# Idle products on TensorE, and a quarter of the last batch's spectral products on POOL

## The chip, the cores and the metric

The kernel runs on one core of a Trainium2 chip, in one launch. The metric is the device time of one execution in microseconds (us). Five engines work side by side, each through its own instructions in order: PE (TensorE, matrix products into PSUM), DVE (VectorE), ACT (ScalarE), POOL (GpSimd) and SP (SyncE, which here only issues DMAs).

## What is computed

For 8 batches of 3136 rows and 256 columns, an attention-like product without softmax feeds a gated long convolution:

```python
scores = matmul(z, z.T) / S                    # S = 3136, z has 64 columns
x      = u * matmul(maximum(scores, 0)**2, v)  # u, v: S x 256
x1, x2, x3 = split(x @ w_proj, 3)              # 256 columns each
conv = irfft(rfft(x2, axis=seq) * rfft(filter_fft, axis=seq))
out  = (x1 * conv * x3) @ w_out
```

Inputs and output are float32; the kernel works in bfloat16 with float32 accumulation.

## The kernel before

The sequence is cut into 7 chunks (`CHUNKS`). For each batch and chunk PE makes blocks of scores into PSUM (`ps_s`), ACT takes the positive part (`R_t`, L1767), DVE or ACT squares it (`A_t`, L1776 and L1774), and PE weighs `v` with it into `ps_o`. DVE multiplies the result by `u` (`xT_t`, L1818). With `wp` PE then makes two gate factors, which ACT copies (L554) and DVE multiplies (`gate_t`, L1160), and the input of the convolution.

The convolution is a transform of 3136 = 64 x 49 points, in two steps, with scratch in HBM (`spec`) between them for the reordering. `dft1` makes the first step. `add_spectrum` makes, for each of 8 groups of frequencies (`g`): the second step (`forward`, two PSUM banks), its eviction to a tile `xh` in SBUF (for the last batch `R_t` and `xh` by turns), the complex product with the filter's spectrum `H` on DVE (L1248), the first inverse step (`inverse`), its eviction, and a write to `spec`. `add_end` loads that back (`conv_in_t`; `A_t` for the last batch, L1006), makes the last inverse step (PE, `T`), multiplies it by the gate (`yT_t`, L1334), multiplies by `w_out` (`wo`), evicts and stores.

The complex product of a group is written as `mul(0)` and `mul(1)`: the spectrum tile (4 x 256 = 1024 elements in each of 128 partitions) times the real or the imaginary part of `H`. In batches 0 to 6 two additions (L1252, L1253) follow on DVE. In the last batch (`final`) they are left out and `inverse2` sums the parts in PSUM instead, with the negated matrices `minus`; there are 16 products of 1024 elements in that batch, all on DVE. The groups of the last batch run when no scores or weighing of another batch are left; in the batches before, they run between those of the following batch.

The order of instructions on every engine is not written by hand. A planner (`Plan`) holds queues of tasks with a cost, dependencies and buffers (`Slots`, `Pairs`, `Singles` for PSUM banks), steps through a time of its own, and at each step starts the task that can start first. PE's queues are S (scores), Q (second transform steps), W (weighing), FA, FB and FZ (projections and output). The times in the planner are guesses which only decide an order; on the chip, an instruction starts when its engine has come to it and its semaphores allow.

The lines that matter: `Plan.go` (L356) picks the next task; `mul` (L1245) with `w_` and `z_` (L1256 to L1258); `inv` (L1260), whose task waits for `z_`; `bank` (L532) gives the PSUM bank of a task; `matmul` (L520) records a product with its bank.

Of the kernel before, what the change touches and what calls it, by code (L numbers as in the profile page):

```python
# [12 lines left out]
P = 128  # L13
# [4 lines left out]
ALU = mybir.AluOpType  # L18
# [10 lines left out]
SPEC_LAG = 1  # L29
LATE_F = 6.0  # L30
LATE_OUT = 2.0
AFTER = (1, 3, 5, 6)
FINAL = (0, 2, 4, 6, 1, 3, 5)
ZP, ZL = 0, 0.0
# [10 lines left out]
def c_act(n):  # L45
    return 0.055 + n * 0.000833
# [6 lines left out]
def c_dve2(n):  # L53
    return 0.068 + n * 0.00052


def c_pe(*ns):
    return sum(n / 2400 + 0.003 for n in ns)
# [123 lines left out]
class Plan:  # L182
# [151 lines left out]
    def pick(self, e):  # L334
# [18 lines left out]
                best = (key, s, task)  # L353
        return best and (best[1], best[2], e)

    def go(self):  # L356
        while True:
            got = []
            x = self.pick_pe()
            if x:  # L360
                got.append((x[0], 0, x[1], "PE", x[2]))
            for i, e in enumerate(self.pend):
                x = self.pick(e)
                if x:
                    got.append((x[0], i + 1, x[1], e, None))
            if not got:
                break
            start, _, task, e, k = min(got, key=lambda g: g[:2])
            if k:
                self.queues[k].remove(task)  # L370
                half = k in ("S", "Q")
                if half != (self.mode == "S") and self.mode:
                    start += 0.096
                    self.quarters, self.quad_run, self.score_run = half and self.soon, 0, 0
                self.score_run += k == "S"
                if k == "Q":
                    self.quad_run += 1
                    if self.score_run and not self.quarters:
                        start += 0.092
                    self.quarters = True  # L380
                self.mode = "S" if half else k
                if k == "W":
                    self.credit = min(self.credit + self.rule(start).pace, 2.0)
                elif k != "S":
                    self.credit = max(self.credit - task.cost["PE"], -2.0)
            self.run(task, e, start)
        left = sum(len(q) for q in self.queues.values()) + sum(len(q) for q in self.pend.values())
        assert not left, f"{left} tasks left over"
# [3 lines left out]
def kernel(  # L392
# [10 lines left out]
    nc = tc.nc  # L403

    B, S, D = u.shape
# [23 lines left out]
    plan = Plan()  # L429
# [90 lines left out]
    def matmul(o, *args, **kw):  # L520
        wrote(nc.tensor.matmul(o, *args, **kw), o)  # L521
# [4 lines left out]
    pair_slots, one_slots, half_slots = Pairs(banks), Singles(banks), Halves(banks)  # L526
# [5 lines left out]
    def bank(dtype=F32):  # L532
        for p in ps_o:
            if plan.bank is p.slots:
                return p.tile()
        i, h = plan.got[0][1]
        x = ps_t[i][:, h, :]
        return x if dtype == F32 else x.bitcast(dtype)
# [9 lines left out]
    def on(engine, emit, cost, deps=(), takes=(), **kw):  # L548
        return job(None, lambda e: emit(), {engine: cost}, deps, takes, **kw)
# [75 lines left out]
    ident = const.tile([P, P], BF16, name="ident")  # L625
# [74 lines left out]
    plan.free["POOL"] = 12.0  # L700
    plan.free["SP"] = 3.0
    plan.free["DVE"] = 1.5


    def after(task, at):
# [12 lines left out]
    for i, (t0, t1) in enumerate(zip(z_cuts, z_cuts[1:])):  # L718
        step_ = -(-(t1 - t0) // -(-(t1 - t0) // 8))
        for g0 in range(t0, t1, step_):  # L720
# [15 lines left out]
            n = nt * dqk  # L736
            at = ZF_AT[i]
# [23 lines left out]
            ev = job(None, back, {"DVE": c_dve2(w), "ACT": c_act(w)}, [tt], prio=0)  # L761
# [17 lines left out]
    H = const.tile([P, NJ, 2, D], BF16, name="H")  # L779
# [163 lines left out]
    minus_task = []  # L943
# [129 lines left out]
    def c_quads(i, n=1):  # L1073
        return n * (1 if i else 2) * c_pe(2 * D) + 0.01
# [139 lines left out]
    def add_spectrum(b, puts):  # L1214
        deps0 = list(h_done) + list(tz_done) if b == 0 else []
        final = b == B - 1
        sets = [(0, 1), (2, 3), (4, 5), (6,), (7,)] if final else [(0, 1), (2, 3), (4, 5), (6, 7)]
        set_of = {g: x for x in sets for g in x}
        outs = [gs_p, gs_p, M_p[2], A_p, uT_p] if final else [gs_p] * 4
        homes = [l_p, l_p, *M_p[:2]]  # L1220
        lasts = []
        behind = []
        ldb, gb = [None], [None]
        for g in range(NJ // 2):
            own = not final or g % 2 == 0
            xh = xh_p if own else R_p
            mine = set_of[g]
            per, gh = 2 * len(mine), outs[sets.index(mine)]
            if g % 2 == 0:
                ldb[0] = load_spec(D1[b % 2], 2 * g, 4, puts, LATE_LOAD * (not final), homes[g // 2] if final else l_p)  # L1230
            ld, ibox = ldb[0]
            xb = {}

            def mm(ps, g=g, xb=xb, ibox=ibox, xh=xh):
                xb["x"] = xh.tile([P, 2, 4, D], BF16)
                forward(ps, slot(ibox["t"], 2 * g % 4), g)

            def ev(e, h, p, xb=xb):
                copy(e, xb["x"][:, 0, ds(2 * h, 2), :].rearrange("p c d -> p (c d)"), p)

            a0, evs = add_quads(mm, ev, c_quads(g), [ld, *deps0], [xh.slots])
            if g % 2:
                a0.frees.append((ld, 0))

            def mul(i, g=g, xb=xb):  # L1245
                x = xb["x"][:].rearrange("p i (j c) d -> p i j c d", c=2)
                h = H[:, ds(2 * g, 2), i].unsqueeze(2).to_broadcast([P, 2, 2, D])
                nc.vector.tensor_tensor(x[:, 1 - i], x[:, 0], h, ALU.mult)  # L1248

            def add(xb=xb):  # L1250
                x = xb["x"][:].rearrange("p i (j c) d -> p i c j d", c=2)
                nc.vector.tensor_tensor(x[:, 1, 0], x[:, 1, 0], x[:, 0, 1], ALU.subtract)  # L1252
                nc.vector.tensor_tensor(x[:, 1, 1], x[:, 1, 1], x[:, 0, 0], ALU.add)  # L1253

            cost = c_dve2(4 * D)
            w_ = on("DVE", lambda mul=mul: mul(0), cost, evs, prio=ZP)  # L1256
            w_ = on("DVE", lambda mul=mul: mul(1), cost, [w_], prio=ZP, lat=ZL)
            z_ = w_ if final else on("DVE", add, 2 * c_dve2(2 * D), [w_], prio=ZP)  # L1258

            def inv(g=g, xb=xb, z_=z_, a0=a0, gh=gh, mine=mine, per=per):  # L1260
                new = g == mine[0]
                if new:
                    gb[0] = {"es": [], "firsts": []}
                gx = gb[0]

                def mm(ps, g=g, new=new):
                    if new:
                        gx["g"] = gh.tile([P, 2 * per, D], BF16)
                    z, y = (slot(xb["x"][:, i], 0) for i in range(2))
                    if final:  # L1270
                        inverse2(ps, y, z, g)
                    else:
                        inverse(ps, y, g)

                def ev(e, h, p, g=g):
                    copy(e, gx["g"][:, ds(2 * (2 * (g - mine[0]) + h), 2), :].rearrange("p c d -> p (c d)"), p)

                a, evs = add_quads(
                    mm, ev, c_quads(g, 1 + final), [z_, *gx["firsts"], *(minus_task if final else [])], [gh.slots] if new else []
                )  # L1280
                gx["firsts"] = [a]
                if new:
                    gx["g0"] = a
                a.frees.append((a0, 1))
                inverses.append(a)
                gx["es"] += evs
                if g != mine[-1]:
                    return
                j0 = 2 * mine[0]

                def put():
                    for rows, part in by_row(D2[b % 2], gx["g"], 2 * j0, 2 * per):
                        nc.sync.dma_start(out=rows, in_=part)

                p_ = on("SP", put, 1.2, gx["es"], moves=0.5 * per, late=LATE_D2 * (not final))
                p_.frees.append((gx["g0"], 1))
                lasts.append(p_)

            behind.append(inv)
            if g >= SPEC_LAG:  # L1300
                behind.pop(0)()
        for x in behind:
            x()
        return lasts

    def add_end(b, lasts, gtasks, cs, kind="FB", src=c_p, dsts=(o_p,), late=0, behind=(), then=(), split=False, mids=(y_p,)):
        for at, c in enumerate(cs):
# [94 lines left out]
            else:  # L1402
                s_ = on("SP", lambda nt=nt, store=store: store(0, nt), 1.3, [*oe, *behind], prio=1, moves=0.45 * nt, late=LATE_OUT * (dst is o_p))
            s_.frees.append((o0, 1))
# [326 lines left out]
    for gi, g in enumerate(groups):  # L1731
        deps = []
        for un in g:
            b, c, k = un
# [7 lines left out]
        more = ends_at.get(gi, [])  # L1742
# [12 lines left out]
        for i, un in enumerate(g):  # L1755
            b, c, k = un
            cw = CHUNKS[c]
            pair = plans[b, c][k][1]
            rows, n = P, len(parts(un))
# [38 lines left out]
            if pair != (NT - 1,):  # L1798
                w_ = add_weigh(un, [q_], lambda t, q_=q_: t.frees.append((q_, 0)))
# [112 lines left out]
```

## Time and profile before

| | |
|---|---|
| three timed runs | 991.3, 991.36, 992.84 us; median 991.36 |
| profiled execution | 993.72 us, of which the span from the first to the last instruction 991.5 |
| busy share of the span | PE 97%, ACT 88%, DVE 83%, POOL 19% |
| mean granted clock of TensorE | 0.990 |
| instructions | 19534 in all, 6831 matrix products, 409 on POOL |

The page's lists and the answers of the trace give, for each group or instruction: source line, engine, operation, tiles out<-in, shape, count; then the busy time and mean duration in ns, and the idle time of the engine before it with what ended it. In the rows in order of time the first number is the start in us from the span's start, the second the time that the row covers. Helpers hold many operations: L521 is every matrix product, L554 and L558 every copy by ACT or DVE, so the tiles' names tell them apart.

### The profile page before, as it was taken

To read this page: it belongs to the slowest core of one execution; us is meant where nothing else is said; L and a number is where in the kernel's file an instruction comes from. 1 tells how busy PE (TensorE), PEld (TensorE's weight loads), DVE (VectorE), ACT (ScalarE), POOL (GpSimd) and SP (SyncE) were. 2 spreads that over 40 slices of the span, in tenths; PEclk is the share of its full clock that TensorE was granted. 3 is DMA by queue.
4 is the path that set the end of the run, shared out by engine and by line. 5 is a ranking of instruction groups with operands and counts; after the bars stand their busy time and mean duration, and the time that the engine had idled before them with its cause. 6 is when DMAs were issued, how large, how long until landed. Compare 5 with 4: busy or idle time off the path is not lost.

```text
span 991.5 us, 19534 instructions
## 1 busy us (share of the span) xinstructions
PE 958.2 (97%) x6831; PEld 472.2 (48%) x6831; DVE 819.4 (83%) x1465; ACT 867.9 (88%) x1187; POOL 191.7 (19%) x409
## 2 busy tenths in 40 slices
PE   6999999999999999999999999999999999999985
PEld 2344544455444554446444454444544455544643
DVE  7876689987899878987789877898779988799774
ACT  6988898988998898899989999889989899999773
POOL 5132311132013210313111220121202231001001
PEclk9999999999999999999999999999999999999978
DMA  9889958979979799978998786998889978984576
GB/s 154 150 171 199 165 118 128 187 137 185 202 174 176 147 194 187 186 156 133 200 197 178 148 152 152 205 191 158 153 196 186 203 138 165 202 213 106 154 229 197
DMA packets 332343, 170.32 MB, mean 172 GB/s; under 512 B 242442, under 2 KB 307786, under 8 KB 332244
## 3 DMA queue, kind: packets, MB, share of 16 engines
q1 hardware_dynamic: 304068, 136.59, 63.4%
q0 software_dynamic: 28176, 32.48, 23.2%
q8 instruction: 54, 0.88, 0.4%
q14 instruction: 45, 0.37, 0.1%
HBM read 90.26 MB, written 53.35 MB: 145 GB/s over the span
## 4 chain that ended last, share of the span: by engine, by line
PE 82%; DVE 7%; ACT 4%; DMA 2%; issue 2%; SPq 1%; POOL 0%; POOLq 0%; DVEq 0%; ACTq 0%
PE ps_o_t L521 48%; PE ps_s L521 34%; DVE A_t L1776 2%; ACT R_t L1767 2%; DVE xT_t L1818 1%; DMA M2e_t<-A_t 1%; DVE xh L1248 1%; DMA ost_t<-in_z_dram 1%; DMA conv_in_t<-spec 1%; DVE gate_t L1160 1%; DVE yT_t L1334 1%; SPq L646 1%; ACT A_t L1774 0%; ACT x_t L554 0%; DMA M_t<-A_t 0%
## 5 line engine op out<-in xcount | busy, mean ns | idle before, releaser
L1767 ACT ACTIVATE R_t<-ps_s 128x1024 f32<-128x1024 f32 (+4 forms) x512 | 466.9, 963 | 57.1 <-PE ps_s L521 55.0
L521 PE MATMUL ps_o_t<-A_t,v_t 128*128 128x512 bf16 (+3 forms) x2084 | 459.5, 354 | 2.9 <-DVE A_t L1776 2.1
L521 PEld LDWEIGHTS <-v_t 128*128 128x128 bf16 (+2 forms) x2878 | 250.6, 98 | 257.8 <-issue 73.2
L1776 DVE TENSOR_TENSOR A_t<-R_t 128x1024 bf16<-128x1024 f32 (+3 forms) x283 | 313.9, 1123 | 64.2 <-ACT R_t L1767 61.1
L1774 ACT ACTIVATE A_t<-R_t 128x1024 bf16<-128x1024 f32 (+3 forms) x213 | 211.7, 1007 | 3.1 <-DMA M2e_t<-A_t 1.7
L521 PE MATMUL ps_s<-zT_t 64*64 64x512 bf16 (+5 forms) x1485 | 170.8, 361 | 2.0 <-ACT R_t L1767 1.0
L604 POOL COPY tick<-xT_t 1x1 bf16<-1x1 bf16 x54 | 13.8, 256 | 681.6 <-DVE xT_t L1818 681.6
L521 PEld LDWEIGHTS <-zT_t 64*64 64x64 bf16 (+1 forms) x1518 | 53.9, 101 | 109.7 <-issue 93.7
L521 PE MATMUL ps_s<-xT_t,wp 128*128 128x512 bf16 (+2 forms) x430 | 103.7, 353 | 2.4 <-DVE gate_t L1160 0.9
L554 ACT ACTIVATE x_t<-ps_s 128x512 bf16<-128x512 f32 (+2 forms) x148 | 81.7, 583 | 19.7 <-PE ps_s L521 12.5
L1818 DVE SCALAR_TENSOR_TENSOR xT_t<-ps_o_t,uT_t 128x256 bf16<-128x256 f32 (+2 forms) x224 | 76.1, 381 | 22.8 <-PE ps_o_t L521 14.4
L1248 DVE TENSOR_TENSOR xh<-xh,H 128x1024 bf16<-128x1024 bf16 x120 | 82.0, 683 | 2.1 <-ACT xh L554 0.9
L521 PE MATMUL ps_o_t<-M_t,v_t 128*128 128x512 bf16 (+2 forms) x352 | 81.8, 353 | 0.0
L1160 DVE TENSOR_TENSOR gate_t<-ps_s,x_t 128x256 bf16<-128x256 f32 (+2 forms) x216 | 71.2, 381 | 6.6 <-PE ps_s L521 4.6
L1334 DVE TENSOR_TENSOR yT_t<-ps_s,gate_t 128x512 bf16<-128x512 f32 (+2 forms) x99 | 57.9, 613 | 10.3 <-PE ps_s L521 10.0
L558 DVE CAST xh<-ps_s 128x512 bf16<-128x512 f32 x71 | 47.3, 685 | 22.8 <-PE ps_s L521 19.5
L521 PEld LDWEIGHTS <-wp 128*128 128x128 bf16 x448 | 42.3, 98 | 49.6 <-issue 15.2
L595 POOL DMA_DIRECT2D un_t<-in_u_dram x112 | 59.8, 554 | 5.6 <-issue 2.7
L614 POOL DMA_DIRECT2D v_t<-in_v_dram x112 | 59.4, 552 | 6.4 <-issue 3.8
L521 PE MATMUL ps_s<-wp,xT_t 128*128 128x256 bf16 x398 | 56.7, 272 | 0.5 <-ACT R_t L1767 0.3
L521 PE MATMUL ps_s<-wo,yT_t 128*128 128x256 bf16 (+1 forms) x344 | 52.0, 273 | 1.6 <-DVE yT_t L1334 1.3
L554 ACT ACTIVATE s_t<-ps_s 128x512 bf16<-128x512 f32 (+1 forms) x79 | 44.9, 592 | 5.5 <-PE ps_s L521 2.1
(154 smaller groups left out, 833.1 us busy)
## 6 DMA issues: line engine op xcount, KB each, us to landing
out_dram<-ost_t SPq DMA_DIRECT2D x66, 256.0 KB
spec<-s_t SPq DMA_DIRECT2D x96, 128.0 KB
spec_in_t<-spec SPq DMA_DIRECT2D x60, 192.0 KB
spec<-gs_t SPq DMA_DIRECT2D x60, 192.0 KB
v_t<-in_v_dram POOLq DMA_DIRECT2D x80, 128.0 KB, 4.5
un_t<-in_u_dram POOLq DMA_DIRECT2D x80, 128.0 KB, 4.9
conv_in_t<-spec SPq DMA_DIRECT2D x33, 256.0 KB
out_dram<-ost_t SPq DMA_DIRECT2D x19, 128.0 KB
```

Of the source, the lines that this page charges most:

```text
L521: wrote(nc.tensor.matmul(o, *args, **kw), o)
L554: got = nc.scalar.activation(out_, in_, AF.Copy)
L558: got = nc.vector.tensor_copy(out_, in_)
L595: nc.gpsimd.dma_start(out=t[ds(j * N1, N1), lo - t0 : hi - t0, :], in_=x[:, n2 : n2 + hi - lo, :])
L614: nc.gpsimd.dma_start(out=t[ds(j * N1, N1), ds(v_at(a), (b - a) * D)], in_=r[:, n2 + a - lo : n2 + b - lo, :].rearrange("p t d -> p (t d)"),)
L1160: got = nc.vector.tensor_tensor(g[:, ::-1] if h == 0 else g, p, x, ALU.mult)
L1248: nc.vector.tensor_tensor(x[:, 1 - i], x[:, 0], h, ALU.mult)
L1334: got = nc.vector.tensor_tensor(yb["y"][:, dh, 0:w], p, gates[b, c, dh][:, 0:w], ALU.mult)
L1767: has_read(nc.scalar.activation(blocks(box["R"], n, cw)[:rows], p, AF.Relu), p)
L1774: nc.scalar.activation(a, r, AF.Square)
L1776: nc.vector.tensor_tensor(a, r, r, ALU.mult)
L1818: nc.vector.scalar_tensor_tensor(x, f, inv_s2, ut, ALU.mult, ALU.mult)
```

## The change

It has two parts. First, the planner may put idle products on PE: `fill` is asked before each task that is started, and if PE would be idle long enough until then it puts a product of the identity with itself (512 columns) into a free single PSUM bank. Up to 13 us of the planner's time this is allowed always, at twice the cost; later only when no scores and no weighing are left in the queues. Nothing reads what these products write. Second, in the last batch `mul(1)` is cut in two: DVE multiplies the first half of the elements (512) and POOL the second half, after `mul(0)`; the inverse step waits for both.

```diff
+WARM, SPARE = 13.0, 0.25
...
+    def fill(self, until):
+        t = self.free["PE"]
+        opening = t < WARM
+        cost = c_pe(512) * (1 + opening)
+        if not opening and (self.queues["S"] or self.queues["W"] or not any(self.queues.values())):
+            return False
+        start = t + 0.096 * (self.mode == "S")
+        if until < start + cost + 0.096 * (self.mode == "S") + SPARE or self.singles.when() > start:
+            return False
+        self.bank, self.got = self.singles, [(self.singles, self.singles.take(start))]
+        self.filler()
+        self.free["PE"] = start + cost
+        self.singles[self.got[0][1]] = start + cost
+        if self.mode:
+            self.mode, self.quarters = "W", False
+        return True
...
             start, _, task, e, k = min(got, key=lambda g: g[:2])
+            if self.fill(start):
+                continue
...
+    plan.free["PE"] = 1.8
+    plan.singles = one_slots
+    plan.filler = lambda: matmul(bank(), ident[:], ident[:].unsqueeze(1).to_broadcast([P, 4, P]), start=True, stop=True)
...
-            def mul(i, g=g, xb=xb):
-                x = xb["x"][:].rearrange("p i (j c) d -> p i j c d", c=2)
-                h = H[:, ds(2 * g, 2), i].unsqueeze(2).to_broadcast([P, 2, 2, D])
-                nc.vector.tensor_tensor(x[:, 1 - i], x[:, 0], h, ALU.mult)
+            def mul(i, at=slice(0, 2), by=nc.vector, g=g, xb=xb):
+                x = xb["x"][:].rearrange("p i (j c) d -> p i j c d", c=2)[:, :, at]
+                n = at.stop - at.start
+                h = H[:, ds(2 * g + at.start, n), i].unsqueeze(2).to_broadcast([P, n, 2, D])
+                by.tensor_tensor(x[:, 1 - i], x[:, 0], h, ALU.mult)
...
             w_ = on("DVE", lambda mul=mul: mul(0), cost, evs, prio=ZP)
-            w_ = on("DVE", lambda mul=mul: mul(1), cost, [w_], prio=ZP, lat=ZL)
-            z_ = w_ if final else on("DVE", add, 2 * c_dve2(2 * D), [w_], prio=ZP)
+            if final:
+                more = on("POOL", lambda mul=mul: mul(1, slice(1, 2), nc.gpsimd), 1.25, [w_])
+                z_ = [on("DVE", lambda mul=mul: mul(1, slice(0, 1)), c_dve2(2 * D), [w_], prio=ZP), more]
+            else:
+                w_ = on("DVE", lambda mul=mul: mul(1), cost, [w_], prio=ZP, lat=ZL)
+            z_ = z_ if final else on("DVE", add, 2 * c_dve2(2 * D), [w_], prio=ZP)
...
-                    mm, ev, c_quads(g, 1 + final), [z_, *gx["firsts"], *(minus_task if final else [])], [gh.slots] if new else []
+                    mm, ev, c_quads(g, 1 + final), [*(z_ if final else [z_]), *gx["firsts"], *(minus_task if final else [])], [gh.slots] if new else []
```

## The prediction

> **What bounds the kernel now.** The page first: TensorE (PE) is busy for 97% of the span and carries 82% of the chain that ended last, so over most of the run only PE's work counts. The clock strip beside it is full except in the last two of 40 slices. The change can therefore do something only at the two ends, and the views by window show what holds them.
>
> ```profile
> PE 82%; DVE 7%; ACT 4%; DMA 2%; issue 2%; SPq 1%; POOL 0%; POOLq 0%; DVEq 0%; ACTq 0%
> PEclk9999999999999999999999999999999999999978
> ```
>
> The order of the built program, changed against before, says the same: up to the last batch's end the PE order differs only by inserted products and by which PSUM bank is used. There are 45 idle products of 512 columns: 12 in the opening, 33 from about 943 us on.
>
> The opening hangs on a transfer, not on PE:
>
> ```profile
> 6.50 6.37 DMA ost_t<-in_z_dram
> 12.90 1.04 ACT xT_t L554 x2
> 13.94 0.95 ACT R_t L1767
> 14.92 1.23 DVE A_t L1776
> ```
>
> In the chain in order of time, the third piece of z lands at 12.87, ACT casts it until 13.94, and only then squares scores.
>
> At the other end, the windows view (us; PE, PEld, DVE, ACT, POOL busy with counts; then the granted clock):
>
> ```profile
> 947.94:951.35 3.41, 1.84 (x40) 1.19 (x42) 3.41 (x7) 2.92 (x7) 0.00 (x0) 1.00 0.98 297
> 951.35:954.76 3.41, 3.14 (x47) 2.10 (x37) 3.41 (x7) 3.09 (x7) 0.00 (x0) 0.50 0.83 271
> 954.76:958.18 3.42, 3.34 (x44) 1.91 (x38) 2.98 (x5) 3.42 (x8) 0.00 (x0) 0.50 0.84 228
> 961.59:965.00 3.41, 3.41 (x26) 1.35 (x16) 1.38 (x2) 2.39 (x4) 0.00 (x0) 0.50 0.49 145
> 965.00:968.40 3.40, 2.91 (x15) 1.33 (x14) 2.36 (x7) 1.36 (x3) 0.00 (x0) 1.00 0.26 75
> ```
>
> PE runs at half clock from 951.35 to 965.0, after a stretch in which it was busy only 1.84 of 3.41 us. But in the first two of these windows VectorE (DVE) is busy 3.41 of 3.41. The groups of that stretch and its first and last product:
>
> ```profile
> L1248 DVE TENSOR_TENSOR R_t<-R_t,H 128x1024 bf16<-128x1024 bf16 x8 | 5.5, 682 | 0.0
> L1248 DVE TENSOR_TENSOR xh<-xh,H 128x1024 bf16<-128x1024 bf16 x8 | 5.5, 681 | 0.0
> L558 DVE CAST gs_t<-ps_s 128x512 bf16<-128x512 f32 x3 | 2.1, 688 | 0.4 <-ACT xh L554 0.4
> 948.59 0.68 DVE L1248 TENSOR_TENSOR xh<-xh,H 128x1024 bf16<-128x1024 bf16 x1
> 949.19 0.68 DVE L1248 TENSOR_TENSOR R_t<-R_t,H 128x1024 bf16<-128x1024 bf16 x1
> 960.61 0.68 DVE L1248 TENSOR_TENSOR R_t<-R_t,H 128x1024 bf16<-128x1024 bf16 x1
> ```
>
> From 948.59 to 961.29, 12.7 us, DVE does 16 products and 4 casts that start 0.60 apart: 20 x 0.60 = 12.0, and the idle is 0.4. So the stage is bound by DVE, and the half clock costs nothing in it. It costs after it, where the gate products of the last batch follow.
>
> **The change part by part.** The sum is made against the profiled execution: 993.72 us, its span 991.5 and 2.2 around it. The median of the three timed runs, 991.36, is 2.4 lower; I carry the difference over to it.
>
> *Opening, 12 idle products.* Seven stand ahead of the first transpose, one and four more behind it, all in PE's wait for z. They may give the early products their full clock sooner, but ACT is not free before 13.94 and its order is unchanged: 0. Were ACT not the cover, scores that started at 13.43 could start about 1.0 us earlier.
>
> ```profile
> 11.40 2.10 PE L521 MATMUL ps_o_t<-A_t,v_t 128*128 128x512 bf16 x6
> 13.43 0.82 PE L521 MATMUL ps_s<-zT_t 64*128 64x512 bf16 x6
> ```
>
> (Six products in 11.40 to 13.43 are 0.34 each; at the full rate below, 0.215, they end about 0.8 to 1.0 sooner.)
>
> *The products: a quarter to POOL.* Eight second products shrink from 1024 to 512 elements on DVE, and eight of 128x512 go to POOL. The half-size price is that of the additions of the batches before:
>
> ```profile
> 896.74 0.41 DVE L1252 TENSOR_TENSOR xh<-xh 128x512 bf16<-128x512 bf16 x1
> 897.08 0.41 DVE L1253 TENSOR_TENSOR xh<-xh 128x512 bf16<-128x512 bf16 x1
> ```
>
> They start 0.34 apart, so DVE's products fall from 16 x 0.60 = 9.6 to 8 x 0.60 + 8 x 0.34 = 7.5. In the same order three evictions move from ACT to DVE (3 x 0.60 = 1.8), so DVE as a whole loses only 0.3.
>
> POOL's price is not in the trace. Its nearest rows are these:
>
> ```profile
> masks.py:199 POOL TENSOR_SCALAR_AFFINE_SELECT yT_t<-yT_t 128x128 f32<-128x128 f32 x1 | 0.3, 295 | 0.1
> L868 POOL MEMSET S<- 128x512 f32 x1 | 0.5, 549 | 0.0
> L604 POOL COPY tick<-xT_t x54: 177/178/1239, 33.9 to 914.1; 1x1 bf16<-1x1 bf16 x54
> ```
>
> A fill of 512 elements, which reads nothing, takes 0.55: the lower bound. Four selects of 128 elements, which read one input, are 4 x 0.295 = 1.18. If a second input costs as much again, 2.4: the upper bound. I take 1.18, since the select is the only row that reads at length, and its fixed part, counted four times, stands for part of the second input. [...]
>
> What decides is whether POOL's product runs beside DVE's. The last row is a copy of one element: 0.178 in the median, 1.239 at most. The long ones:
>
> ```profile
> 127.15 1.21 DVE L1776 TENSOR_TENSOR A_t<-R_t 128x1024 bf16<-128x1024 f32 x1
> 127.17 1.24 POOL L604 COPY tick<-xT_t 1x1 bf16<-1x1 bf16 x1 [9.44 <-DVE xT_t L1818]
> 278.59 0.68 DVE L1248 TENSOR_TENSOR xh<-xh,H 128x1024 bf16<-128x1024 bf16 x1
> 278.77 0.55 POOL L604 COPY tick<-xT_t 1x1 bf16<-1x1 bf16 x1 [16.76 <-DVE xT_t L1818]
> ```
>
> At 127.17 the copy starts 0.02 behind a DVE product with both inputs in SBUF and ends 0.05 after it (128.41 against 128.36). At 278.77 it starts inside one of the very products L1248 and ends 0.05 after it (279.32 against 279.27). So POOL, reading SBUF, waits for the end of such a DVE product. The other direction, a DVE product that waits for a running POOL product, no row shows, since a one-element copy is too short. I take it to hold: the two do not read at once, so the products of both engines go one after another. Time for them: 7.5 + 8 x 1.18 = 9.4, together 16.9 us, against the 12.7 that the stage takes now: **+4.2**. DVE's casts read PSUM and can lie beside POOL. [...] Walking the two orders, that loses nothing if POOL starts only in the holes that DVE leaves, and about 2.0 if the two alternate (three casts in a row stand before the fifth product, 3 x 0.60, with nothing ready for POOL): I take **+1.0**. The three moved evictions are hidden in this. Each inverse transform waits for its POOL product as well; on POOL's own queue only the last six stores stand behind the eight, and they come later.
>
> [...]
>
> *The 33 idle products at the end.* Eleven stand in gaps before 949.3 (waits for yT and for the products), five between inverses. Three of them stand ahead of a forward transform that starts at 948.03, and delay it by 3 x 0.215 = 0.65; its consumer, the third pair of products, is by then behind POOL in any case: 0. Of the rest, 13 stand in a row between the last gate product (`wp`) and the first inverse transform of the output (`T,A_t`), three behind it.
>
> ```profile
> 962.39 1.89 PE L521 MATMUL ps_o_t<-xT_t,wp 128*128 128x512 bf16 x4
> 964.07 1.49 PE L521 MATMUL ps_s<-xT_t,wp 128*128 128x512 bf16 x4
> 966.04 1.02 PE L521 MATMUL ps_s<-xT_t,wp 128*128 128x512 bf16 x4 [0.48 <-DVE gate_t L1160]
> 966.90 1.03 PE L521 MATMUL ps_o_t<-xT_t,wp 128*128 128x512 bf16 x4
> 970.45 0.43 PE L521 MATMUL ps_s<-xT_t,wp 128*128 128x320 bf16 x2
> 970.72 0.39 PE L521 MATMUL ps_s<-T,A_t 128*128 128x128 bf16 x4
> 971.72 1.28 DVE L1334 TENSOR_TENSOR yT_t<-ps_s,gate_t 128x512 bf16<-128x512 f32 x2
> 972.46 0.38 PE L521 MATMUL ps_s<-T,A_t 128*128 128x128 bf16 x4 [0.21 <-DVE yT_t L1334]
> 972.92 0.68 DVE L1334 TENSOR_TENSOR uT_t<-ps_s,gate_t 128x512 bf16<-128x512 f32 x1
> ```
>
> Four products of 512 columns take 0.86 at full clock (966.04 to 966.90), 0.215 each, and 1.68 at half (962.39 to 964.07), 0.42 each. Before, `T,A_t` follows the last `wp` directly, with no idle time named: its data had landed. So 13 x 0.215 = 2.8 us come in front of it. DVE used its result 1.0 later (971.72), held by its own gates, where 0.46 is enough (972.46 to 972.92); that slack of 0.5 absorbs a part: **+2.3**. PE is in order, so everything behind the 13 waits: the output products, their evictions, the stores. The three later ones lie beside two DVE products: 0.
>
> *The clock behind the stage.* Eight `wp` took 962.39 to about 965.5 at half clock. With a longer stage of which PE is idle the more, I expect half clock there again, so no gain; if the clock held, 8 x 0.2 = 1.65 would go.
>
> Sum: 4.2 + 1.0 + 2.3 = **+7.5**: 1001.2 against 993.72, and on the median 991.36 + 7.5 = **998.9**.
>
> **The rivals.** *Worse than that (slower).* Strict alternation (+2.0 instead of 1.0) and the 13 at half clock (13 x 0.42 = 5.5, less 0.5) give 4.2 + 2.0 + 5.0 = +11.2: 1002.6. For it: two `wp` groups in the stretch after the stage were cold; against it: they ended the half clock within 3 us.
>
> *POOL is not held, nor holds.* Then DVE decides: 7.5 + 7 casts x 0.60 = 11.7 from 948.59, end 960.3; POOL's last product follows the last whole product (0.94 before that) by 1.18 and a handover, 960.6, so -0.7. With the 13 it is +1.6: 993.0; with the clock held (-0.4 and -1.65, below), 990.9. For it: the missing row for DVE behind POOL. Against: the two copies.
>
> *Faster: the clock holds.* The idle products keep the clock at 1.00 through 951 to 965. Place: the opening's scores (-1.0), the last inverse (16 products of 256 columns at half clock, 961.34 to 962.39; -0.4), the `wp` (-1.65): -3.05, 988.3. It decides only if POOL delays nothing and the loads of `A_t` land so late that the 13 hide behind them; against that is the `T,A_t` of 970.72 that waited for no load.
>
> ```profile
> 961.34 0.48 PE L521 MATMUL ps_s<-R_t,TZ 64*64 64x256 bf16 x4
> ```
>
> **How the numbers follow.** Chances: forecast 0.62 with its spread of POOL's price, worse 0.13, not held 0.18, faster 0.07. POOL at 0.8 us a product would make it +4.5 (995.9), at 1.6 +10.9 (1002.3). The range, 990.5 to 1003.5, takes in most of the "not held" case and leaves out the faster one, a bit of "not held" and the dearest POOL. A comparison can tell about 0.2%, 2.0 us, from no change: 989.4 to 993.3. Faster gets 0.07, and 0.01 of "not held"; same gets 0.15 of "not held"; the rest, 0.77, is slower.
>
> **What would show it.** Right: DVE's L1248 rows in the last batch, or POOL's new rows, much longer than 0.68 and 1.18, the long ones of one engine ending where one of the other ends; the first to the last product some 18 us instead of 12.7; 13 idle products directly before `T,A_t`, without a wait for a load. Wrong: products of both engines side by side at their own lengths; a clock of 1.00 from 951 to 965; `T,A_t` waiting for `A_t` although 13 products stand before it.

## Result, and the profile after

Six runs of the changed kernel gave 997.55 to 999.82 us, median 998.72; six of the kernel before 990.8 to 993.27, median 991.75. The ratio is 1.0057 with a 95% interval of 1.0046 to 1.0069: slower by 5.7 us (4.6 to 6.8). The two medians lie 7.0 apart. The profiled execution took 997.61 us with a span of 995.8.

Where the time went is read from landmarks that both traces have (us from the span's start; the profiled executions, 993.72 and 997.61):

| | before | after | difference |
|---|---|---|---|
| start to DVE's first product of the last batch | 948.59 | 947.61 | -1.0 |
| from there to the end of DVE's last product | 12.70 | 17.80 | +5.1 |
| from there to the first gate product of the output (`yT_t`) | 10.43 | 9.99 | -0.4 |
| from there to the span's end | 19.8 | 20.4 | +0.6 |

The first row says nothing of the change: in the last experiment below, whose edit touches only writes of the last batch, the products began at 950.90. The page looks as before, with the chain on PE and the clock full but for the last two slices:

```profile
PE 82%; DVE 7%; ACT 4%; issue 3%; DMA 2%; SPq 1%; POOLq 0%; POOL 0%; DVEq 0%; ACTq 0%
PEclk9999999999999999999999999999999999999978
```

So it is the end again that has to be read, and there the stage of the products lost 5.1 us, most of what the whole comparison lost. First POOL and then DVE in order of time, in the changed kernel (start, time, then engine, line, operation, tiles, shape, count):

```profile
948.44 1.46 POOL L1272 TENSOR_TENSOR xh<-xh,H 128x512 bf16<-128x512 bf16 x1 [33.72 <-DVE xh L1272]
949.87 1.32 POOL L1272 TENSOR_TENSOR R_t<-R_t,H 128x512 bf16<-128x512 bf16 x1
952.16 1.39 POOL L1272 TENSOR_TENSOR xh<-xh,H 128x512 bf16<-128x512 bf16 x1 [0.96 <-DVE xh L1272]
954.17 1.15 POOL L1272 TENSOR_TENSOR R_t<-R_t,H 128x512 bf16<-128x512 bf16 x1 [0.63 <-DVE R_t L1272]
```

```profile
948.20 0.69 DVE L1272 TENSOR_TENSOR R_t<-R_t,H 128x1024 bf16<-128x1024 bf16 x1
948.80 1.38 DVE L1272 TENSOR_TENSOR xh<-xh,H 128x512 bf16<-128x512 bf16 x1
950.11 1.37 DVE L1272 TENSOR_TENSOR R_t<-R_t,H 128x512 bf16<-128x512 bf16 x1
...
952.46 1.64 DVE L1272 TENSOR_TENSOR R_t<-R_t,H 128x1024 bf16<-128x1024 bf16 x1
954.01 0.68 DVE L578 CAST gs_t<-ps_s 128x512 bf16<-128x512 f32 x1
```

POOL's first product begins inside a DVE product that ends at 948.89, and takes 1.46 instead of the 1.15 that it takes beside a cast (954.17). DVE's half product, 0.41 in the kernel before, begins at 948.80, in POOL's, and takes 1.38: it ends 0.28 after POOL's end at 949.90. The whole product of 952.46 ends 0.55 after POOL's (953.55). So in these rows a product that overlaps one of the other engine ends after it by nearly its own length (POOL's by 1.01 of 1.15, DVE's by 0.28 of 0.41 and 0.55 of 0.68), as if it waited for the other's end first. DVE's cast, which reads PSUM, keeps its 0.68. The same by groups of the stage:

```profile
L1272 POOL TENSOR_TENSOR xh<-xh,H 128x512 bf16<-128x512 bf16 x4 | 5.3, 1332 | 37.4 <-DVE xh L1272 37.4
L1272 POOL TENSOR_TENSOR R_t<-R_t,H 128x512 bf16<-128x512 bf16 x4 | 5.1, 1273 | 2.6 <-DVE R_t L1272 2.6
```

```profile
L1272 DVE TENSOR_TENSOR R_t<-R_t,H 128x512 bf16<-128x512 bf16 x4 | 4.7, 1179 | 0.0
L1272 DVE TENSOR_TENSOR R_t<-R_t,H 128x1024 bf16<-128x1024 bf16 x4 | 3.7, 920 | 0.0
L1272 DVE TENSOR_TENSOR xh<-xh,H 128x512 bf16<-128x512 bf16 x4 | 3.4, 851 | 0.0
L1272 DVE TENSOR_TENSOR xh<-xh,H 128x1024 bf16<-128x1024 bf16 x4 | 2.7, 679 | 0.0
```

On each of the two tiles half as many elements take DVE longer (1179 against 920 ns on `R_t`, 851 against 679 on `xh`). DVE shows no idle time in these groups: the wait lies inside the instructions.

The view by windows (busy us and count of PE, PEld, DVE, ACT, POOL, then the granted clock) and PE behind the stage:

```profile
950.12:953.53 3.41, 1.66 (x26) 1.07 (x26) 3.38 (x5) 2.25 (x5) 2.45 (x2) 1.00 0.90 306
953.53:956.94 3.41, 2.19 (x38) 1.71 (x41) 3.41 (x6) 0.84 (x2) 1.17 (x2) 0.50 0.58 185
960.36:963.77 3.41, 3.41 (x31) 1.31 (x32) 3.41 (x5) 1.20 (x2) 2.65 (x2) 0.50 0.20 71
963.77:967.20 3.43, 2.65 (x38) 1.20 (x30) 2.93 (x5) 1.78 (x4) 1.15 (x1) 1.00 0.46 133
```

```profile
965.92 1.04 PE L541 MATMUL ps_o_t<-xT_t,wp 128*128 128x512 bf16 x3
966.79 1.03 PE L541 MATMUL ps_s<-xT_t,wp 128*128 128x512 bf16 x4
...
971.34 0.71 PE L541 MATMUL ps_o_t<-xT_t,wp 128*128 128x320 bf16 x4
971.88 3.26 PE L541 MATMUL ps_s<-ident 128*128 128x512 bf16 x13
974.98 0.61 PE L541 MATMUL ps_s<-T,A_t 128*128 128x128 bf16 x8
```

The half clock lasts 10.2 us, from 953.53 (before: 13.7), and is over at 963.77, before the first `wp`: four of them take 0.87 where the first four took 1.68. The 13 idle products stand in front of `T,A_t`, as expected, but what stands ahead of them is so much quicker that `yT_t` starts 0.4 nearer to the last product than before. In pieces, against before: from the last product to the first `wp` 0.51 instead of 1.10 us (the last inverse transform at full clock), from there to the first of the 13 (before: to `T,A_t`) 5.96 instead of 8.33, the 13 themselves 3.10, and from `T,A_t` to `yT_t` 0.42 instead of 1.00: -0.59 - 2.37 + 3.10 - 0.58 = -0.44.

### The profile page after: what moved, and what is told of

Read it like the earlier page. It is cut to its first block, busy times and chain, and to the rows that moved or that the text cites. A ratio compares the mean times of both kernels' runs of the same rounds, so it can differ in the third digit from the quotient of the medians.

```text
span 995.8 us, 19538 instructions
## 1 busy us (share of the span) xinstructions
PE 958.0 (96%) x6775; PEld 474.8 (48%) x6876; DVE 825.6 (83%) x1468; ACT 866.4 (87%) x1184; POOL 201.8 (20%) x417
## 4 chain that ended last, share of the span: by engine, by line
PE 82%; DVE 7%; ACT 4%; issue 3%; DMA 2%; SPq 1%; POOLq 0%; POOL 0%; DVEq 0%; ACTq 0%
PE ps_o_t L541 48%; PE ps_s L541 34%; ACT R_t L1795 2%; DVE A_t L1804 2%; DVE xT_t L1846 1%; DVE xh L1272 1%; DVE yT_t L1362 1%; DMA specf<-s_t 1%; DMA ost_t<-in_z_dram 1%; ACT x_t L574 1%; SPq L666 1%; DVE gate_t L1183 0%; DMA M_t<-A_t 0%; ACT A_t L1802 0%; DVE gs_t L578 0%
## 5 line engine op out<-in xcount | busy, mean ns | idle before, releaser
L541 PE MATMUL ps_o_t<-A_t,v_t 128*128 128x512 bf16 (+4 forms) x2003 | 445.0, 353 | 8.8 <-issue 4.7
L624 POOL COPY tick<-xT_t 1x1 bf16<-1x1 bf16 x54 | 13.7, 255 | 680.6 <-DVE xT_t L1846 680.6
L541 PE MATMUL ps_s<-xT_t,wp 128*128 128x512 bf16 (+2 forms) x410 | 99.8, 352 | 2.4 <-issue 0.5
L1362 DVE TENSOR_TENSOR yT_t<-ps_s,gate_t 128x512 bf16<-128x512 f32 (+2 forms) x99 | 58.0, 616 | 13.7 <-PE ps_s L541 13.5
L541 PEld LDWEIGHTS <-wp 128*128 128x128 bf16 x448 | 41.9, 98 | 47.1 <-issue 11.7
```

Source lines behind the costliest of these rows:

```text
L1362: got = nc.vector.tensor_tensor(yb["y"][:, dh, 0:w], p, gates[b, c, dh][:, 0:w], ALU.mult)
```

## Experiments

Theories: (A) the two engines' products wait for each other because both read SBUF; this is the loss. (B) The idle products are the loss. (C) Not the reading, but POOL's length, the handovers or another order. Differences below are against before in the same comparison, by the ratio.

**The idle products alone.**

```diff
-                more = on("POOL", lambda mul=mul: mul(1, slice(1, 2), nc.gpsimd), 1.25, [w_])
-                z_ = [on("DVE", lambda mul=mul: mul(1, slice(0, 1)), c_dve2(2 * D), [w_], prio=ZP), more]
+                z_ = [on("DVE", lambda mul=mul: mul(1), cost, [w_], prio=ZP, lat=ZL)]
```

> The idle products stay (48 of them: 12 in the opening, 17 small groups in the last batch's second steps, 16 in a row before the first inverse transform of the output, 3 behind it); the products of spectrum and filter are all on DVE again. Theory (the shared reading of DVE and POOL costs the time): the stage from the first to the last product of the last batch is 12.7 us again, within 0.3, and the 16 cost 16 x 0.215 - 0.5 = +2.9, against which stands the full clock on the gate products if it comes earlier (up to -2.0): +0.9 to +2.9 against before, 992.7 to 994.7. Rival (the idle products are what costs, POOL nothing): +5 to +7, about 998. Second rival (the idle products hold the clock and the 16 hide behind loads): -2.0, 989.8.

Median 993.99, ratio 1.0008 (0.9999 to 1.0017): +0.8 us, just under the theory's lower edge. B, at +5 to +7, is out. The stage takes 12.1 us, 0.3 less than the theory allowed. The profiled execution, 996.38, is the slowest of the eleven; in it seven of the idle products in the gaps, at half clock, hold the next inverse transform until 963.03, though DVE's last product for it ended at 961.66. So a product in a gap can stand in the way as well.

**POOL's quarter alone.**

```diff
-            if self.fill(start):
-                continue
-    plan.free["PE"] = 1.8
```

> No idle products anywhere; POOL makes its quarter of the products as in the changed kernel. Theory (the products of DVE and POOL go one after another): the stage takes 17 to 18 us instead of 12.7, POOL's products 1.15 each where nothing is in the way and up to 1.5 beside a DVE product, and without the 13 idle products the step from the last product to the first gate product of the output is shorter than in the changed kernel by up to 2.3, unless the gate products are at half clock again: +3 to +5 against before, 995 to 997. Rival (idle products cost, POOL nothing): as before, 991.75 within 0.2%, with a stage of 12 to 13 us.

Median 997.8, ratio 1.0051 (1.0037 to 1.0065): +5.1 us. From DVE's first product to POOL's last it is 17.8 us, with the same prolonged rows as in the changed kernel. The clock is the other half of this experiment; PE after the stage, and a late window:

```profile
968.55 1.89 PE L539 MATMUL ps_o_t<-xT_t,wp 128*128 128x512 bf16 x4
970.23 3.00 PE L539 MATMUL ps_s<-xT_t,wp 128*128 128x512 bf16 x8
```

```profile
965.48:968.90 3.42, 2.56 (x29) 1.22 (x29) 2.04 (x5) 0.97 (x3) 1.32 (x1) 0.50 0.53 152
```

Without idle products the half clock lasts 20.5 us, from 951.6 to 972.1, and the first `wp` run at half clock. Over all runs the mean granted clock says the same: its median is 0.987 here, 0.990 to 0.991 in the changed kernel, 0.993 before, 0.995 with idle products alone. Over the whole traces of before and of the changed kernel, windows of 0.2 us show 1.00 and 0.50, and values between them only where the clock changes inside a window. So (1 - clock) x 2 x span is an estimate of the time at half clock: 25.9, 18.9, 13.9 and 9.9 us. (For the trace of before, at 0.990, it gives 19.8; its windows at half clock are 951.35 to 965.0 and 985.48 to the span's end, 19.7.)

**Both, without the products at the end** (neither the 13 before `T,A_t` nor the 3 behind).

```diff
+        if t > 960.0:
+            return False
```

> As the changed kernel, without the 13 idle products before the first inverse transform of the output and the 3 behind it. Theory (the 13 are on the path): the changed kernel's 998.7 less 2.3 = 996.4; the distance from the last product to the first gate product of the output falls from 10.0 to about 7.7 us. Rival (the 13 hide behind the gates or loads): 998.7 as it was, the distance 10.0 within 0.3.

Median 997.06, ratio 1.0039 (1.0026 to 1.0052), 1.8 us below that of the changed kernel, though the intervals overlap. From the last product to `T,A_t` it is 7.6 us instead of 9.6, to `yT_t` 8.0 instead of 10.0 (expected: 7.7), and PE waits for something new:

```profile
973.42 0.62 PE L543 MATMUL ps_s<-T,A_t 128*128 128x128 bf16 x8 [0.96 <-DMA A_t<-spec]
```

So 13 x 0.215 = 2.8 us of idle products cost 2.0: the rest lies in a wait of 0.96 for the load from the scratch, which shows once the `wp` are quick.

**The idle products alone, without those at the end** (both edits above together).

> Idle products only in the opening (12) and between the second steps of the last batch (17), none before or behind the first inverse transform of the output; all products of spectrum and filter on DVE. Theory (the idle products before the end are worth what they do to the clock): if the gate products that follow the stage run at full clock, -1.65 to -2.0 against before, 989.8 to 990.1; if the half clock of 951 to 965 stays, as before, 991.75 within 0.2%. Between the two I lean to the second, since a dozen idle products in gaps of the stage make PE little busier there. Rival (idle products cost by themselves, wherever they stand): 1 to 3 us slower than before.

Median 992.31, ratio 0.9998 (0.9988 to 1.0007): no change is seen, although the gate products run at full clock from 961.57, for which -1.65 to -2.0 was expected. Part of the gain goes into a wait for the load:

```profile
961.57 1.04 PE L543 MATMUL ps_o_t<-xT_t,wp 128*128 128x512 bf16 x4
...
966.99 0.71 PE L543 MATMUL ps_o_t<-xT_t,wp 128*128 128x320 bf16 x4
969.19 0.62 PE L543 MATMUL ps_s<-T,A_t 128*128 128x128 bf16 x8 [1.49 <-DMA A_t<-spec]
```

The chain in order of time shows what holds that load:

```profile
961.68 0.58 ACT uT_t L576
962.26 1.04 ACT x_t L576 x2
963.30 0.28 SPq L1322
963.59 0.04 issue
963.63 2.70 DMA spec<-uT_t
...
966.47 2.67 DMA A_t<-spec
```

A write of 2.70 and a load of 2.67 through HBM; the last eviction ends at 962.4 (DVE's half: 961.71, 0.69), but SP issues the write at 963.3, since it is busy with the three transfers of the group before until 963.15.

The wait is not the whole account. By the landmarks of this trace `yT_t` starts 8.57 us after the last product, with the wait in it, instead of 10.43 before, and the stage is 0.6 shorter. The gain is lost behind `yT_t`: from there to the end it is 21.97 us instead of 19.78, and the clock is at half for 3.4 us there (in the last columns the granted clock, the share of the DMA engines and GB/s):

```profile
970.00:972.00 2.00, 1.41 (x11) 1.07 (x12) 1.51 (x3) 0.00 (x0) 0.00 (x0) 0.67 0.86 242
972.00:974.00 2.00, 2.00 (x15) 1.60 (x14) 0.97 (x2) 1.19 (x2) 0.00 (x0) 0.50 0.81 243
```

In the trace of the POOL write below, where the products there take their time at full clock (four `wo` products 0.60 from 969.88 on, against 1.01 from 970.97 on here), that stretch takes 20.96; so about 1.0 of the 2.2 goes with the half clock, and the rest stays open.

**Fills in place of POOL's products.** POOL's quarter of the products is left out.

```diff
-                more = on("POOL", lambda mul=mul: mul(1, slice(1, 2), nc.gpsimd), 1.25, [w_])
+                more = on("POOL", lambda xb=xb: [nc.gpsimd.memset(xb["x"][:, 0, 2:4], 0.0) for _ in range(2)], 1.25, [w_])
```

> As the changed kernel, but POOL's quarter of the products is left out: in its place POOL fills the same 512 elements twice with zero, which takes about as long (2 x 0.55) and reads nothing; the inverse transform waits for it as before. Theory (POOL's and DVE's products stand in each other's way by reading SBUF): DVE's half products fall from up to 1.6 to 0.42, the stage from 17.8 to 12 to 13 us, and the time from 998.7 to 993 to 994. Rival (POOL's length, its handovers or the planner's order cost the time, not the reading): the stage stays at 17 to 18 us, the time at 998.

Median 992.64, ratio 0.9999 (0.9984 to 1.0015): all of the loss is gone; 993 to 994 was expected. POOL is as long on each group, and DVE's half products lie beside it at their own length:

```profile
948.90 1.11 POOL L1282 MEMSET xh<- 128x512 bf16 x2 [33.69 <-DVE xh L1272]
949.96 1.11 POOL L1282 MEMSET R_t<- 128x512 bf16 x2
```

```profile
948.70 0.68 DVE L1272 TENSOR_TENSOR R_t<-R_t,H 128x1024 bf16<-128x1024 bf16 x1
949.30 0.41 DVE L1272 TENSOR_TENSOR xh<-xh,H 128x512 bf16<-128x512 bf16 x1
949.64 0.41 DVE L1272 TENSOR_TENSOR R_t<-R_t,H 128x512 bf16<-128x512 bf16 x1
```

The stage is 11.9 us long, with PE's and DVE's instructions in the same order as in the changed kernel and the inverse transforms waiting for POOL as there. C is out. What costs is that POOL reads SBUF beside DVE's products: the stage took 17.8 us with its reads and takes 11.9 with its fills.

**The 12 idle products of the opening alone,** all products of spectrum and filter on DVE.

```diff
+        if not opening:
+            return False
```

> Only the 12 idle products of the opening; no others, and no product on POOL. Theory (the transfer of z and then ACT hold the opening): as before within 0.2%. Rival one (they give the first products their full clock sooner): -1.0. Rival two (the clock that was granted early falls to a half for 3.4 us a little later, from 15 to 18 us, and costs there what it saved): 0 to +1.0; the strip of the clock shows which.

Median 993.31, ratio 1.0009 (0.9998 to 1.0021): a loss of up to 2 us or none, not to be told apart by time. The traces side with the second rival. PE in the opening, first before, then here:

```profile
14.94 0.96 PE L524 MATMUL ps_s<-ident,xT_t 128*128 128x128 bf16 x13 [0.69 <-ACT R_t L1767]
18.39 2.16 PE L521 MATMUL ps_o_t<-A_t,v_t 128*128 128x512 bf16 x8 [0.41 <-DVE A_t L1776]
20.48 0.82 PE L521 MATMUL ps_s<-zT_t 64*128 64x512 bf16 x6
```

```profile
14.92 0.96 PE L546 MATMUL ps_s<-ident,xT_t 128*128 128x128 bf16 x13 [2.77 <-ACT R_t L1796]
18.82 2.56 PE L543 MATMUL ps_o_t<-A_t,v_t 128*128 128x512 bf16 x8
21.31 0.82 PE L543 MATMUL ps_s<-zT_t 64*128 64x512 bf16 x6
```

PE is early and waits 2.77 for ACT instead of 0.69; at 14.9 the two are level. The clock falls after that wait, for 3.4 us from 16.8 on, and the products there are slow: PE is 0.83 behind at 21.31.

```profile
16.20:19.70 3.50, 3.50 (x13) 0.89 (x13) 3.50 (x6) 2.12 (x3) 0.48 (x2) 0.58 0.78 109
```

The changed kernel has such a half clock from 14.9 to 18.3. The clock's record is doubtful in the first microseconds: before, it reads 1.00 from 11 to 13 us, though six products take 0.34 each there, against 0.23 each here, behind the idle products.

**The last write issued by POOL,** added to the kernel of the fourth experiment (idle products alone, none at the end), and then without those of the opening.

```diff
-                p_ = on("SP", put, 1.2, gx["es"], moves=0.5 * per, late=LATE_D2 * (not final))
+                p_ = on("POOL" if end else "SP", put, 1.2, gx["es"], moves=0.5 * per, late=LATE_D2 * (not final))
```

(`end` is the last group of the last batch; `put` uses `nc.gpsimd` there.)

> As the kernel with idle products up to the last gate products and none behind, all products on DVE, with one thing more: the write of the last group of the last batch to the scratch is issued by POOL, which is idle there, instead of SP, where it stood behind the three transfers of the group before it (SP's queue started it 0.9 us after its data was there). Theory (the way through the scratch, write 2.7 us and load 2.7 us, is what holds the first inverse transform of the output once the gate products run at full clock): the wait for the load falls from 1.5 to about 0.6 us, the time by 0.9 against that kernel, to 991.4, or -1.1 against before. Rival (a transfer that POOL issues lands later, or the gate products are next): no gain, 992.3.

> As the kernel with the last write issued by POOL, without the 12 idle products of the opening; 17 idle products in the last batch alone. Theory (those of the opening do nothing): the same as with them, 991.4, within 0.2%. Rival (they cost about 0.5 to 1.0 by the half clock that follows them): 990.5 to 991.

Ratios 0.9997 (0.9987 to 1.0007) and 0.9995 (0.9984 to 1.0006). The first misses its 0.9. The releaser that the trace names for POOL is the landing of an earlier write to the same scratch,

```profile
962.07 1.59 POOL L1325 DMA_DIRECT2D spec<-uT_t  x3 [46.90 <-DMA spec<-M2o_t]
```

so POOL starts 0.56 after the last eviction (961.51) and 1.9 after DVE's last product, where SP started 2.2 after it, and `T,A_t` still waits 1.31. The second does not tell whether the opening costs anything: the medians, 992.86 and 992.02, are 0.8 apart with overlapping intervals.

**The 17 gap products alone; with one write for the last two groups; that write alone.** The first leaves the fourth experiment's opening out; then the edit for the write:

```diff
-        if t > 960.0:
+        if t > 960.0 or opening:
             return False
```

```diff
-        sets = [(0, 1), (2, 3), (4, 5), (6,), (7,)] if final else [(0, 1), (2, 3), (4, 5), (6, 7)]
+        sets = [(0, 1), (2, 3), (4, 5), (6, 7)] if final else [(0, 1), (2, 3), (4, 5), (6, 7)]
-        outs = [gs_p, gs_p, M_p[2], A_p, uT_p] if final else [gs_p] * 4
+        outs = [gs_p, gs_p, M_p[2], M_p[0]] if final else [gs_p] * 4
```

> Only the 17 idle products between the second steps of the last batch and the first gate products behind it; none in the opening, none before or behind the first inverse transform of the output, no product on POOL, SP issues all writes. Theory (they keep the clock through the stage, and what the gate products gain by it is given back at the load through the scratch): as before within 0.2%, on the side of faster by 0.2 to 0.8; the first inverse transform waits 1.3 to 1.5 for its load. Rival (the gap products are worth the whole clock gain once the opening is left alone): -1.6 to -2.0 against before.

> As the kernel with the 17 gap products alone, and the two last groups of the last batch are written to the scratch in one go (3 transfers instead of 6), so that SP, which was busy with the first of the two writes, issues it as soon as the last eviction is there. Theory (the way through the scratch is the bound after the stage): the write starts 0.85 us earlier, the wait for the load falls from 1.4 to about 0.5, and the time by 0.85 against that kernel: 1.1 to 1.6 faster than before, about 991.2. Rival (a write of double size lands later, or the gates' last products on DVE are next): 0 to -0.3 against the kernel with the gap products alone.

> As before, with no idle product and nothing on POOL; only the two last groups of the last batch are written to the scratch in one go. Theory (before, the gate products at half clock are what ends last, and the load is there in time): the same as before within 0.2%. Rival (the load is the bound before too): -0.5 to -0.85.

| | median | ratio |
|---|---|---|
| gap products | 991.51 | 0.9990 (0.9977 to 1.0003) |
| gap products and one write | 990.02 | 0.9976 (0.9964 to 0.9988) |
| one write | 993.02 | 0.9997 (0.9987 to 1.0008) |

Gap products and one write together beat both kernels, by 2.4 us (1.2 to 3.6) against before; 1.1 to 1.6 was expected. Alone, neither is told from no change. Why the pair gains is not settled. With the gap products alone the wait for the load is 1.27; with one write the chain has:

```profile
962.52 0.50 ACT x_t L576
963.02 0.11 SPq L1322
...
963.17 2.84 DMA spec<-M_t
...
966.07 2.77 DMA A_t<-spec
...
968.88 0.41 PE ps_s L543 x4
```

The last eviction ends at 962.77, so from there to `T,A_t` it is 6.1 us, against 6.6 (961.90 to 968.46) with the gap products alone: of the 0.85 expected, 0.45 is there, because write and load take 0.23 longer each (2.84 and 2.77 against 2.61 and 2.54). In this execution a half clock from 956.3 to 959.7 made the last evictions late (the last ends 1.8 us after DVE's last product, against 1.3 with the gap products alone), and hid even that: from the last product to `yT_t` it is 8.36 us, and 8.33 with the gap products alone. The two traces differ behind it, 19.59 against 21.71 us from `yT_t` to the end, where in the other a half clock from 970.7 to 974.1 slowed the output products. The mean granted clock of the runs is 0.996 with both edits and 0.995 without the second. How much of the gain is the write and how much the clock stays open.

## Why the prediction was right, and where it was off

*Products not at once.* Right, both ways: the copies in the trace of before showed POOL behind DVE (the copy ends at 128.41, DVE at 128.36), and the changed kernel shows DVE behind POOL (1.38 for 0.41), which had been assumed. With POOL's products, which read SBUF, beside DVE's, which have two inputs there, the time grew by 5.1 us (POOL's quarter alone, ratio 1.0051), and with POOL's fills, which only write, by nothing (0.9999).

*Sizes.* POOL's 1.18 was 1.15. The term with its loss by order, 4.2 + 1.0, came out as 17.80 - 12.70 = 5.1; the 1.0 was the author's estimate, and no run shows it by itself, only the sum. Part of that closeness is luck, since with all products on DVE the stage took between 12.10 and 13.29 us in the traces; but POOL alone costs 5.1 by the ratio as well, over all runs. The rival "not held" had 11.7 us for the stage; with fills in place of reads it is 11.9.

*"The half clock costs nothing in it."* Off by 0.6: with the same DVE order and the clock full through most of the stage (opening products alone) it takes 12.10, 20 steps of 0.60 without the idle gaps of before. In the trace of the one write alone, at half clock in 953.1 to 959.9, it takes 13.29, and DVE sits idle there for PE (0.56) and ACT (0.44).

*The 13 products, +2.3.* They cost 2.0 in the profile with the rest of the changed kernel around them. Its reason, "its data had landed", holds for before, where slow `wp` hid the load, but not for the changed kernel: with quick `wp` there is a wait of about 1.0, and the products cover it.

*"I expect half clock there again, so no gain."* This is the step that failed. It holds for POOL's quarter without idle products (half clock to 972.1); with the idle products between the inverses the half clock ended at 963.77, and near 963.4 without the products at the end (there by PE's rows: four products of 256 columns take 0.43 from 962.47 on, 0.28 from 963.78 on), each time before the `wp`. The last inverse and the `wp`, put at 0.4 and 1.65 if the clock held, became 0.6 and 2.4 us quicker (the order of the later `wp` changed too and may hold a part), and this stands against the 13: from the last product to `yT_t` it is -0.4 instead of +2.3. All idle products together cost 0.8 (-0.1 to 1.7) by the experiment.

*The opening, 0.* ACT was the cover, as said (14.92 and 14.94). Missed was what the early PE did next: it idled longer (2.77 instead of 0.69), and a half clock of 3.4 us followed. What that costs in all, no run tells from nothing.

*Sum.* The +7.5 was 0.5 above the difference of the medians and 1.8 above that of the ratio, and by parts it should have been 5.1 to 5.2 for the products and some 0.8 for the idle ones, 6.0. That 998.9 fell on 998.72 is partly luck. The profile of before had a mean clock of 0.990, the low end of the 0.989 to 0.995 that its runs showed later, so it has more half clock than usual (19.8 us against 13.9).

## What to carry to other kernels

Before work is given from DVE to POOL, see what both read at that moment: here, with two DVE inputs in SBUF and POOL reading SBUF too, the times added up (a stage of 17.8 us instead of 12.7), and the only sign was longer instructions (1.38 us instead of 0.41), not waits. Idle products in gaps ahead of a stretch that PE bounds went with a fuller clock (0.995 against 0.993 in the mean), though alone they brought no gain that the runs can tell from none; where they stood on the path they cost most of their length (2.0 of 2.8 us), and a PE that was early and then waited (2.77 us) had a half clock right behind it (3.4 us); after a gain, read what the next instruction now waits for, and mend that too.

## What the hardware showed beyond this

- The prolonged instructions took the rest of the other's and then nearly their own length: DVE's half product took 1.38 for 0.41, POOL's 1.46 for 1.15.
- The half clock came in pieces of 3.4 us (changed kernel, from 14.87 on), 6.8 (the one write alone, by the lengths of PE's products), 10.2 (changed kernel, from 953.53 on), 13.7 (before, from 951.35 on) and 20.5 (POOL's quarter alone, from 951.6 on); a further piece reached the span's end (6.0 us before, 8.1 in the changed kernel). The first five are near 1, 2, 3, 4 and 6 times 3.41, the first one's length. The time at half clock differed between executions of one kernel: the mean clock of the kernel before went from 0.989 to 0.995.
- A write issued on POOL waited, by the releaser that the trace names, for the landing of an earlier write to the same scratch that SP had issued (at 961.96; POOL starts at 962.07). With SP issuing both (idle products alone, none at the end) the last write follows 0.11 us after the issuing of the one before it ended, at 963.26.
